# Block 0 of a chunked linear attention with a gated feed-forward: fewer fill-in matrix products, a later fourth q transpose, and two outputs ahead of the first gate product

## The chip, the core and the metric

One core of a Trainium2 chip runs the whole program. The core has a matrix engine (TensorE, "PE" in the profile, with its weight loads as "PEld"), a vector engine (VectorE, "DVE"), a scalar engine (ScalarE, "ACT"), GpSimd ("POOL"), and SyncE ("SP"), which here only issues transfers. Each engine [...] waits on semaphores for the others. The metric is the device time of one execution in microseconds (us); the kernel before takes 224.36 us (median of 6 runs, 223.84 to 224.38).

## The reference

A linear attention with a decay per head runs over blocks of the sequence, and its output is the input of a feed-forward layer with a sigmoid gate:

```python
# q, k, v: (B=4, H=8, S=768, D=64); lam: (8,)
for each block of the sequence:
    intra = (qb @ kb.T * Dmask) @ vb              # Dmask[i, j] = lam ** (i - j) for i >= j
    inter = (qb * lam ** (i + 1)) @ kv_state
    out   = intra + inter
    kv_state = lam ** block * kv_state + (kb * lam ** (block - 1 - i)).T @ vb
x    = out as (B * S = 3072 tokens, H * D = 512)
gate = sigmoid(x @ w_gate)                        # w_gate, w_val: (512, 1536)
y    = (gate * (x @ w_val)) @ w_out               # w_out: (1536, 512), y: (3072, 512)
```

Any block length gives the same result, and the kernel uses 128 positions. In the first block the state is zero, so only the intra part is computed there.

## The kernel before, in words

**Blocks.** The sequence is cut into 6 blocks of 128 positions (`NSTEP`), each for all 4 batches, which gives 512 tokens for the feed-forward per block. A block's attention output is kept transposed as `XT[n]`, 128 partitions x 2 batch pairs x 4 parts of the model dimension x 256 tokens. The feed-forward of a block goes over 12 column tiles of `w_gate` and `w_val` (`piece_gv`, lines 562 to 576): four products for the gate (`gp`), four for the value (`vp`), a tanh on ScalarE, and the product of both on VectorE. Then `piece_po` (line 588) multiplies by `w_out`.

**Block 0.** It is written out by hand in lines 614 to 649, ahead of everything else on TensorE, and it is where the change lies. For each batch b there are these steps:

- `t_0("k", b)` and `t_0("q", b)` (line 282) transpose k and q by eight products with an identity matrix into PSUM. `e_0` (line 337) copies the result to SBUF as `KS` and `QS`, on ScalarE, or on VectorE for q of batches 0 and 1.
- `s_0(b)` (line 291) forms the scores in 16 small products, `sp`; VectorE multiplies them with the decay mask in two instructions (line 304) and writes `MT`.
- `a_0(b, engines)` (line 306) multiplies `MT` with v in 16 small products, `op`, and the engines named copy the result to `XT[0]` (line 320). Batches 0 and 1 are the first half of `XT[0]`, batches 2 and 3 the second.

Ahead of these, `cast_hw` (line 363) turns k of batches 0 and 1, which was loaded in FP32, into bf16 on VectorE. The other loads of q, k, v and the weights are issued from GpSimd's queue, in the order of lines 171 to 198.

**Fill-in products.** `zeros(m, dt)` (line 609) issues m products of zeros, 128 x 512 each, into a PSUM tile that nothing reads. They depend only on the memset of the zeros (line 174).

**First products of the feed-forward.** For the first column tile of block 0 the order is split by halves of `XT[0]`: gate on the first half, value on the first half, gate on the second, value on the second. The gate on the first half is issued by hand at line 647; the other three come from `piece_gv`, with

```python
order = [(gp, WG, first), (vp, WV, first), (gp, WG, second), (vp, WV, second)][1 - n:]
```

which leaves the first entry out for block 0.

**Order.** The order of the instructions on each engine is the order in which they are written. The work behind block 0's attention is a list of units with work attached to each (lines 685 to 804), and nothing in it is touched.

Of the kernel before, what the change touches and what calls it, by code (L numbers as in the profile page):

```python
# [8 lines left out]
FP32 = mybir.dt.float32  # L9
# [7 lines left out]
def kernel(  # L17
# [11 lines left out]
    nc = tc.nc  # L29
# [54 lines left out]
    def rows_of(u):  # L84
        return slice(u * 64, (u + 1) * 64)
# [136 lines left out]
    def powers(w):  # L222
        nc.scalar.activation(mask0[:, w], mask0[:, w], AF.Exp)
# [58 lines left out]
    def t_0(c, b, pool=ps_at, tag="ps"):  # L282
        ps = pool.tile([128, 1, HP, C], BF16, name="t" + c, tag=tag)
        for a in range(2):
            for e in range(2):
                for w in range(2):
                    nc.tensor.transpose(ps[rows_of(w), 0, 2 * a + e, :],
                                        T_[c, 0][:, b, 2 * (2 * a + w) + e, :], ident)
        (tqs if c == "q" else tks)[0, b] = ps

    def s_0(b):
        sp = [ps_at.tile([128, HP, C], FP32, name=f"sp{w}", tag="ps") for w in range(2)]
        for a in range(2):
            for e in range(2):
                for w in range(2):
                    for g in range(2):
                        nc.tensor.matmul(sp[w][rows_of(g), 2 * a + e, :],
                                         lhsT=KS[0, b][rows_of(w), 2 * a + e, rows_of(g)],
                                         rhs=QS[0, b][rows_of(w), 2 * a:2 * a + 2, rows_of(g)],
                                         start=(a == 0 and e == 0), stop=(a == 1 and e == 1),  # L300
                                         skip_group_check=True)
        MT[0, b] = mtp.tile([128, 2, HP, C], BF16, tag="MT", name="MT")
        for w in range(2):
            nc.vector.tensor_tensor(out=MT[0, b][:, w], in0=sp[w], in1=mask0[:, w], op=ALU.mult)

    def a_0(b, engs):
        n = len(engs)
        ops = [ps_at.tile([128, HP // n, C], FP32, name="op", tag="ps") for _ in range(n)]
        for r in range(HP):
            for e in range(2):  # L310
                for g in range(2):
                    o, i = divmod(r, HP // n)
                    nc.tensor.matmul(ops[o][rows_of(g), i, :], lhsT=T_["v", 0][rows_of(g), b, 2 * r + e, :],
                                     rhs=MT[0, b][rows_of(g), r % 2, 2 * (r // 2) + e, :],
                                     start=(i == 0 and e == 0), stop=(i == HP // n - 1 and e == 1),
                                     skip_group_check=True)
        if b == 0:
            new_xt(0)
        for o, eng in enumerate(engs):
            (eng.tensor_copy if eng is nc.vector else eng.copy)(  # L320
                XT[0][:, b // 2, o * (HP // n):(o + 1) * (HP // n), b % 2 * C:(b % 2 + 1) * C], ops[o])
# [15 lines left out]
    def e_0(c, b, eng):  # L337
        es = QS if c == "q" else KS
        if b % 2 == 0:
            t = trsb.tile([128, 2, HP, C], BF16, tag=c.upper() + "S", name=c.upper() + "S")  # L340
            for i in range(2):
                es[0, b + i] = t[:, i]
        (nc.scalar.copy if eng is nc.scalar else nc.vector.tensor_copy)(
            es[0, b], (tqs if c == "q" else tks)[0, b][:, 0])
# [18 lines left out]
    def cast_hw(b):  # L363
        nc.vector.tensor_copy(T_["k", 0][:, b], H32[:, b])
# [52 lines left out]
    def new_xt(n):  # L417
        XT[n] = xtp.tile([128, 2, NMT, TCH // 2], BF16, tag="XT", name="XT")
# [133 lines left out]
    def product(n, ft, ps, W, part):  # L552
        fs = slice(ft * 128, (ft + 1) * 128)
        for mt in range(NMT):
            nc.tensor.matmul(ps[:, part], lhsT=W[:, mt, fs], rhs=XT[n][:, part, mt],  # L555
                             start=(part is not second and mt == 0),
                             stop=(part is not first and mt == NMT - 1), skip_group_check=True)

    def new_gv(n, ft):
        GV[n, ft] = [ps_ff.tile([128, 2, TCH // 2], FP32, name=c, tag="ff") for c in ("gp", "vp")]  # L560
# [48 lines left out]
    def zeros(m, dt=BF16):  # L609
        z = nought if dt is FP32 else ST[1, 0].rearrange("p a h j d -> p (a h j d)")  # L610
        for _ in range(m):
            nc.tensor.matmul(zps, lhsT=z[:, 0:128], rhs=z[:, 0:DM], start=True, stop=True)  # L612
# [2 lines left out]
    powers(0)  # L615
    exponents(1)
    powers(1)
    zeros(2, FP32)
    zeros(3)
    cast_hw(0)  # L620
    cast_hw(1)
    t_0("k", 0)
# [10 lines left out]
    s_0(1)  # L633
    t_0("k", 3, ps_ff, "ff")
    e_0("k", 3, nc.scalar)
    zeros(1)
    for b in range(2, 4):
        t_0("q", b)
        e_0("q", b, nc.scalar)
    zeros(1)  # L640
    s_0(2)
    a_0(0, (nc.scalar,))
    a_0(1, (nc.scalar,))
    s_0(3)
    zeros(1)
    new_gv(0, 0)
    product(0, 0, GV[0, 0][0], WG, first)
    a_0(2, (nc.scalar,))
    a_0(3, (nc.scalar, nc.vector))

# [182 lines left out]
```

## Time and profile before

| What | us |
|---|---|
| device time, median of 6 runs | 224.36 |
| device time of the profiled execution | 224.34 |
| its span, first to last instruction | 222.6 |
| PE busy | 216.8 |
| ACT busy | 107.9 |
| DVE busy | 103.7 |
| POOL busy | 64.7 |

The profiled execution is one of the same kernel with the hardware profiler on; its span lies inside its device time, with 1.74 us around it. Starts in the lines of the timeline are in us from the start of the span. In a merged line the second number is the time from the first start to the last end, and "x8" means eight instructions. The ends of products are modelled, with about 0.2 us of pipeline behind the last start, so that lines overlap. The number in brackets is the idle time of the engine just before, with what ended it.

### The profile page before, as it was taken

To read this page: it belongs to the slowest core of one execution; us is meant where nothing else is said; L and a number is where in the kernel's file an instruction comes from. 1 tells how busy PE (TensorE), PEld (TensorE's weight loads), DVE (VectorE), ACT (ScalarE), POOL (GpSimd) and SP (SyncE) were. 2 spreads that over 40 slices of the span, in tenths; PEclk is the share of its full clock that TensorE was granted. 3 is DMA by queue.
4 is the path that set the end of the run, shared out by engine and by line. 5 is a ranking of instruction groups with operands and counts; after the bars stand their busy time and mean duration, and the time that the engine had idled before them with its cause. 6 is when DMAs were issued, how large, how long until landed. Compare 5 with 4: busy or idle time off the path is not lost.

```text
span 222.6 us, 5459 instructions
## 1 busy us (share of the span) xinstructions
PE 216.8 (97%) x2310; PEld 107.6 (48%) x2310; DVE 103.7 (47%) x192; ACT 107.9 (48%) x236; POOL 64.7 (29%) x85
## 2 busy tenths in 40 slices
PE   7989999999999999999999999999999999999994
PEld 2564444557444544444544444544444544444443
DVE  4854575539777501785700785700676400333300
ACT  5748764594384523385433376342366342333221
POOL 7999755740392008402910030000000000000000
PEclk9999999999999999999999999999999999999999
DMA  6999999999899999997999994012100012100022
GB/s 116 177 179 185 196 199 182 167 156 158 140 86 158 255 209 155 181 195 95 98 159 200 210 67 32 3 50 94 47 3 0 0 53 94 47 0 1 3 94 96
DMA packets 99401, 25.27 MB, mean 114 GB/s; under 512 B 90032, under 2 KB 96432, under 8 KB 99376
## 3 DMA queue, kind: packets, MB, share of 16 engines
q0 software_dynamic: 77872, 13.90, 78.0%
q1 hardware_dynamic: 20688, 10.69, 19.9%
q10 hardware_dynamic: 816, 0.33, 0.6%
q8 instruction: 18, 0.29, 0.5%
q14 instruction: 7, 0.06, 0.1%
HBM read 28.32 MB, written 6.29 MB: 155 GB/s over the span
## 4 chain that ended last, share of the span: by engine, by line
PE 92%; POOL 4%; DMA 3%; issue 1%; ACT 0%; POOLq 0%
PE po L595 28%; PE gp L555 28%; PE vp L555 28%; DMA WV<-in_moe_w_val_dram 3%; POOL vb L114 1%; PE sp L455 1%; PE cp L515 1%; PE op L479 1%; POOL qb L114 1%; PE op L493 1%; POOL kb L114 1%; PE sp L381 0%; PE op L412 0%; PE tk L279 0%; PE tq L279 0%
## 5 line engine op out<-in xcount | busy, mean ns | idle before, releaser
L550 DVE SCALAR_TENSOR_TENSOR ht<-sg,vp 128x512 bf16<-128x512 f32 x72 | 49.4, 686 | 93.1 <-PE vp L555 87.4
L555 PE MATMUL vp<-XT,WV 128*128 128x512 bf16 (+1 forms) x296 | 74.3, 373 | 0.7 <-DMA WV<-in_moe_w_val_dram 0.7
L555 PE MATMUL gp<-XT,WG 128*128 128x512 bf16 (+1 forms) x296 | 74.3, 373 | 0.2 <-ACT XT L320 0.2
L573 ACT ACTIVATE sg<-gp 128x512 f32<-128x512 f32 x72 | 43.0, 597 | 59.4 <-PE gp L555 59.4
L595 PE MATMUL po<-WO,ht 128*128 128x512 bf16 (+2 forms) x300 | 63.9, 371 | 0.0
L555 PEld LDWEIGHTS <-WV 128*128 128x128 bf16 x296 | 28.9, 98 | 34.1 <-DMA WV<-in_moe_w_val_dram 0.9
L595 PEld LDWEIGHTS <-ht 128*128 128x128 bf16 x300 | 28.3, 98 | 31.9
L555 PEld LDWEIGHTS <-WG 128*128 128x128 bf16 x296 | 28.2, 98 | 31.7 <-issue 0.4
L599 ACT ACTIVATE ob<-po 128x512 f32<-128x512 f32 (+1 forms) x24 | 14.0, 583 | 38.6 <-PE po L595 38.6
L143 ACT ACTIVATE kd<-kb,kds 128x128 bf16<-128x128 bf16 x80 | 25.2, 389 | 0.0
L674 POOL COPY gates<-qt 128x1 bf16<-128x1 bf16 x4 | 1.5, 386 | 50.0 <-DMA qt<-qb 50.0
L505 ACT CAST XT<-op 128x512 bf16<-128x512 f32 x16 | 8.2, 600 | 5.0 <-PE op L493 5.0
L465 DVE TENSOR_TENSOR MT<-sp,mask 128x512 bf16<-128x512 f32 x16 | 10.3, 682 | 0.0
L96 POOL DMA_DIRECT2D vb<-in_v_dram x6 | 9.0, 1503 | 3.0 <-issue 1.4
L102 POOL DMA_DIRECT2D qb<-in_q_dram x10 | 8.8, 893 | 2.9 <-DMA WO<-in_moe_w_out_dram 2.9
L102 POOL DMA_DIRECT2D kb<-in_k_dram x10 | 9.0, 919 | 1.0 <-DMA WG<-in_moe_w_gate_dram 0.6
L612 PE MATMUL zps<-st 128*128 128x512 bf16 (+1 forms) x10 | 6.2, 748 | 1.5 <-DVE st L174 1.5
L121 POOL DMA_DIRECT2D WV<-in_moe_w_val_dram x9 | 7.4, 836 | 0.0
L118 POOL DMA_DIRECT2D WG<-in_moe_w_gate_dram x8 | 6.8, 848 | 0.0
L540 DVE SCALAR_TENSOR_TENSOR st<-st,pow_l,cp 128x128 bf16<-128x128 bf16 x24 | 6.7, 342 | 0.0
L96 POOL DMA_DIRECT2D kb<-in_k_dram x5 | 5.9, 1184 | 1.2 <-DMA WG<-in_moe_w_gate_dram 1.2
L96 POOL DMA_DIRECT2D qb<-in_q_dram x5 | 5.8, 1153 | 0.5 <-DMA WO<-in_moe_w_out_dram 0.5
(93 smaller groups left out, 125.5 us busy)
## 6 DMA issues: line engine op xcount, KB each, us to landing
out_dram<-ob SPq DMA_DIRECT2D x19, 256.0 KB, 2.0
vb<-in_v_dram POOLq DMA_DIRECT2D x4, 512.0 KB, 7.0
qb<-in_q_dram POOLq DMA_DIRECT2D x14, 128.0 KB, 7.5
kb<-in_k_dram POOLq DMA_DIRECT2D x12, 128.0 KB, 9.1
WO<-in_moe_w_out_dram POOLq DMA_DIRECT2D x4, 384.0 KB, 12.1
kb<-in_k_dram POOLq DMA_DIRECT2D x5, 256.0 KB, 8.9
qb<-in_q_dram POOLq DMA_DIRECT2D x5, 256.0 KB, 8.4
WG<-in_moe_w_gate_dram POOLq DMA_DIRECT2D x4, 256.0 KB, 7.0
```

The source lines that it names most:

```text
L96: nc.gpsimd.dma_start(out=T_[c, n][:, b0:nat], in_=src[b0:nat, :, sl, :].rearrange("b h s d -> s (b h) d"))
L102: nc.gpsimd.dma_start(out=T_[c, n][:, m:b1, u::2, :], in_=src[m:b1, 1 - u::2, sl, :].rearrange("b h s d -> s (b h) d"))
L118: nc.gpsimd.dma_start(out=WG[:, :, f0 * 128:f1 * 128], in_=wg_r[:, :, f0 * 128:f1 * 128])
L121: nc.gpsimd.dma_start(out=WV[:, :, f0 * 128:f1 * 128], in_=wv_r[:, :, f0 * 128:f1 * 128])
L143: nc.scalar.mul(KD[n][:, at, i, :], T_["k", n][:, at, i, :], kds[:, min(n // FIRST_XBAR, 1), h:h + 1])
L465: nc.vector.tensor_tensor(out=MT[n, bp][:, u], in0=SP[n, bp][u], in1=mask[:, u ^ bp].unsqueeze(1).to_broadcast([128, 2, HP, L]), op=ALU.mult)
L505: nc.scalar.copy(XT[n][:, bp].rearrange("p m (j c i) -> p m j c i", j=2, c=2)[:, :, :, c, :], OP[n, c, bp])
L550: return nc.vector.scalar_tensor_tensor(out=o, in0=g, scalar=1.0, in1=x, op0=ALU.add, op1=ALU.mult)
L555: nc.tensor.matmul(ps[:, part], lhsT=W[:, mt, fs], rhs=XT[n][:, part, mt], start=(part is not second and mt == 0), stop=(part is not first ...
L573: nc.scalar.activation(sg, gp.rearrange("p a b -> p (a b)"), AF.Tanh, scale=0.5)
L595: nc.tensor.matmul(po[:, :c1 - c0], lhsT=HT[n, ft][:, tt * 128:(tt + 1) * 128], rhs=WO[:, ft, c0:c1], start=(ft == 0), stop=(ft == NFT - 1))
L599: (eng.mul if eng is nc.scalar else eng.tensor_scalar_mul)(o, po[:, :c1 - c0], 0.5)
```

## The change

Four things change, all between lines 614 and 649:

- At the start, two FP32 and three bf16 fill-in products become one FP32 product.
- Two of the later fill-in products, one on each side of the q transposes of batches 2 and 3, are gone. The last one, behind `s_0(3)`, stays.
- The transposes of q of batch 3, with their copy, move from ahead of `s_0(2)` to behind it.
- `a_0(2)` and `a_0(3)`, with their copies, move ahead of the gate product on the first half.

```diff
@@ -615,8 +615,7 @@
     powers(0)
     exponents(1)
     powers(1)
-    zeros(2, FP32)
-    zeros(3)
+    zeros(1, FP32)
     cast_hw(0)
     cast_hw(1)
     t_0("k", 0)
@@ -633,20 +632,19 @@
     s_0(1)
     t_0("k", 3, ps_ff, "ff")
     e_0("k", 3, nc.scalar)
-    zeros(1)
-    for b in range(2, 4):
-        t_0("q", b)
-        e_0("q", b, nc.scalar)
-    zeros(1)
+    t_0("q", 2)
+    e_0("q", 2, nc.scalar)
     s_0(2)
+    t_0("q", 3)
+    e_0("q", 3, nc.scalar)
     a_0(0, (nc.scalar,))
     a_0(1, (nc.scalar,))
     s_0(3)
     zeros(1)
+    a_0(2, (nc.scalar,))
+    a_0(3, (nc.scalar, nc.vector))
     new_gv(0, 0)
     product(0, 0, GV[0, 0][0], WG, first)
-    a_0(2, (nc.scalar,))
-    a_0(3, (nc.scalar, nc.vector))
```

No load, no work of GpSimd and no order of instructions on VectorE or ScalarE is different; the order changes on TensorE alone.

## The prediction

> **What bounds the kernel now.** I read the page first: TensorE is busy for 97% of the span. Then the waits of TensorE from 15 us to the end, to see whether anything behind the changed stage could absorb a shift.
>
> ```profile
> span 222.6 us, 5459 instructions
> PE 216.8 (97%) x2310; PEld 107.6 (48%) x2310; DVE 103.7 (47%) x192; ACT 107.9 (48%) x236; POOL 64.7 (29%) x85
> ```
>
> ```profile
> PE vp L555 <- DMA WV<-in_moe_w_val_dram: 0.7, 1, 0.7
> ```
>
> The second fence is the whole answer: behind 15 us TensorE waits once, 0.7 us, for the first tile of `w_val`. From there to its last product it doesn't wait again. So the start of the first value product is a gate: what delays it delays the end by as much, and nothing that only makes work ahead of it earlier gains anything. The timeline of TensorE up to there:
>
> ```profile
> 1.53 5.06 PE L612 MATMUL zps<-st 128*128 128x512 f32 x7 [1.53 <-DVE st L174]
> 6.68 0.64 PE L287 MATMUL tk<-ident,kb 128*64 128x128 bf16 x8
> 7.20 0.43 PE L287 MATMUL tq<-ident,qb 128*64 128x128 bf16 x8
> 7.45 0.41 PE L287 MATMUL tk<-ident,kb 128*64 128x128 bf16 x8
> 7.67 0.41 PE L287 MATMUL tq<-ident,qb 128*64 128x128 bf16 x8
> ...
> 12.76 0.39 PE L612 MATMUL zps<-st 128*128 128x512 bf16 x1
> 13.31 0.60 PE L555 MATMUL gp<-XT,WG 128*128 128x256 bf16 x4 [0.16 <-ACT XT L320]
> 13.84 1.08 PE L313 MATMUL op<-MT,vb 64*64 64x128 bf16 x32
> 15.65 0.61 PE L555 MATMUL vp<-XT,WV 128*128 128x256 bf16 x4 [0.73 <-DMA WV<-in_moe_w_val_dram]
> ```
>
> The chain of work that ended last says when the `w_val` tile came: its transfer runs from 9.66 for 5.94 us, to 15.60.
>
> ```profile
> 9.66 5.94 DMA WV<-in_moe_w_val_dram
> ```
>
> And the mask multiplications on VectorE, which feed the outputs:
>
> ```profile
> 8.66 2.48 DVE L304 TENSOR_TENSOR MT<-sp,mask 128x512 bf16<-128x512 f32 x4
> 11.68 2.48 DVE L304 TENSOR_TENSOR MT<-sp,mask 128x512 bf16<-128x512 f32 x4 [0.53 <-PE sp L297]
> ```
>
> **The pace of TensorE.** The timeline shows a second thing. The first eight transposes keep the engine from 6.68 to 7.20, 0.52 us; the same eight later take 0.25 and 0.22. The fill-in products agree: in narrow windows of the timeline the FP32 ones start at 1.53, 2.54, 3.40 and 4.25 (two per product, 0.85 apart), the bf16 ones at 5.53 and 5.96, 0.43 apart for 512 columns, while the four whole gate products later take 0.86, or 0.215 each. So TensorE runs at half pace until about 7.2 us and at full pace from there. The listing of the fill-in line shows the extremes:
>
> ```profile
> L612 PE MATMUL zps<-st x10: 389/634/1222, 1.5 to 12.8; 128*128 128x512 bf16 x6, 128*128 128x512 f32 x4
> ```
>
> A bf16 product takes 389 ns late and 634 ns early. The clock column reads 1.00 in these first windows, so the change of pace has to be read from the starts.
>
> [...]
>
> **The change part by part.**
>
> *Fill-in at the start.* Removed: one FP32 (2 x 0.85) and three bf16 products (3 x 0.43), 3.0 us at half pace. As work they cost nothing: the first transpose waits for the cast of k, which ends at 6.66 (6.20 plus one of two casts of 0.46). The remaining product ends at about 3.3, and TensorE idles from there to 6.66. The removal frees nothing[...]. So I take half pace from 6.68 on[...]. That is the price of this edit.
>
> *Fill-in in the middle.* Two bf16 products, 0.22 us each at full pace. They stood in the queue ahead of the q transposes and of the third scores. Removing them, with the fourth q moved back (another 0.22), lets the third scores start up to 0.2 us earlier: ScalarE's copy of q had 0.17 us of idle time. Everything gained is ahead of the gate at 15.60: worth 0.
>
> *Outputs ahead of the gate product.* Before, the first gate product (0.44 us) ran at 13.31, in the time in which v of batches 2 and 3 was still under way (issued up to 9.06, 4.6 us to landing, 13.7). Now it comes behind the last output. At full pace: outputs of batch 2 from 13.7, batch 3 done at about 14.65, gate product to 15.1, half a microsecond ahead of `w_val`. Cost 0, but the cover shrinks: what delays the last output by more than 0.5 us is now paid in full, where before there was 0.73.
>
> *Half pace through the attention.* Eight transposes or 16 scores take 0.43 instead of 0.22, 16 outputs 0.86 instead of 0.44, and a result is ready 0.2 us behind that. Durations on the other engines are those of before (copies 0.56 to 0.64, mask pair 1.25, two pairs 2.48). Replayed in the new order, with the waits on the copies:
>
> - k0, q0, k1, q1 at 6.68, 7.11, 7.54, 7.97, to 8.40; the scores of batch 0 8.40 to 8.83, before 8.14.
> - k2 to 9.26, scores of batch 1 to 9.69, k3 to 10.12, q2 to 10.55. VectorE's first four multiplications 9.1 to 11.6.
> - ScalarE copies k2 at 9.5, k3 at 10.4 and q2 at 10.95, done 11.5. Third scores 11.55 to 11.98, multiplied 12.25 to 13.5 (before from 11.68).
> - q3 to 12.41, outputs of batches 0 and 1 to 14.13, fourth scores to 14.56, their result 14.8, multiplied 14.8 to 16.08 (before to 14.16).
> - Fill-in to 14.99, outputs of batch 2 to 15.85; outputs of batch 3 wait for 16.08 and end at 16.96.
> - Gate product on the first half 0.44 at full pace: the value product starts at 17.40. That is 17.40 - 15.65 = 1.75 us late.
>
> No transfer is late there, since all were due for 15.65 and the chain has none behind it. So the end moves by 1.75.
>
> *When the clock turns.* Turned by 12.0, the fourth scores end by 13.35, the last mask at 14.8, the gate product at about 15.7: 0.1 late. Turned at 14.1: last mask 15.9, gate product done 16.85, 1.2 late. At 17.0: 1.75. From there each further us costs 0.5, because the gate stage then runs at half pace.
>
> [...] Scores and outputs become dense only at about 11.55[...]. I take 17: 1.75 us.
>
> **Sum.** 0 for the removed work, 0 for the two moves, 1.75 for the clock: span 222.6 + 1.75 = 224.35, and with the 1.74 around the span 226.1. The profiled execution (224.34) stands at the median (224.36), so no correction.
>
> **Rivals.**
>
> *The pace turns in time, or the delay is hidden.* The transposes and scores from 6.68 to 10.55 keep TensorE occupied without a gap. [...] then the gate at 15.60 hides it all: 224.2 to 224.5. This is the rival that isn't slower; it decides at 12.0 us, as worked out above. [...]
>
> *Only the gate products turn it.* The small products use 64 x 64 tiles [...]: 227.8 to 229.5, middle 228.6. [...] Against: transposes and small products did hold the pace from 7.2 to 13.
>
> *A gain.* The middle fill-ins and the fourth q held the third scores. It would need the value product ahead of 15.65, so an earlier `w_val`; its queue is GpSimd's, whose order is the same, and its transfers run without a gap. Bound: 223.9.
>
> **How the numbers follow.** Turned at 13 to 19 us: 0.57, 225.0 to 227.1, with 226.1 the likeliest. In time or hidden: 0.14. Late: 0.23. A gain of over 0.2%: 0.06. The least that a measurement of this kernel tells from no change is about 0.2%, 0.45 us. The first and third case are slower, 0.80; the second is within, 0.14. The range leaves the gain, part of the hidden case and the upper half of the late case out: 224.3 to 228.6.
>
> **What would show it.** Right: transposes of k0, q0, k1, q1 start 0.43 apart; the third scores near 11.55; the last mask ends near 16; the value product starts near 17.4 with no wait for `w_val`; gate products take 0.86 from there. Hidden: the starts tighten to 0.22 before 12 us, and the wait for `w_val` at 15.60 is still there. Late: four gate products take 1.7 us for a stretch. Wrong altogether: full pace at 7.2 as before[...].

## The result

The changed kernel takes 225.77 us (median of 18 runs, 224.71 to 226.75) against 224.40 us before (median of 40 runs, 223.84 to 224.58): a ratio of 1.0064, with a 95% interval of 1.0050 to 1.0077. It is slower by about 1.4 us. But no execution took the median's time: nine lie between 224.71 and 225.16 (the earlier group, median 224.99) and nine between 226.39 and 226.75 (the later group, median 226.62). Against 224.40 that is 0.6 and 2.2 us. The profiled execution (224.99, span 223.2) is one of the earlier group.

The page after, its span and busy times:

```profile
span 223.2 us, 5445 instructions
PE 214.6 (96%) x2303; PEld 107.6 (48%) x2303; DVE 103.5 (46%) x192; ACT 108.0 (48%) x236; POOL 63.5 (28%) x85
```

TensorE is busy for 2.2 us less, and the span is 0.6 us longer. All waits of TensorE after (total, count, longest):

```profile
PE tk L287 <- DVE kb L364: 3.0, 1, 3.0
PE zps L612 <- DVE st L174: 1.5, 1, 1.5
PE sp L297 <- ACT QS L343: 0.8, 1, 0.8
PE op L313 <- DVE MT L304: 0.3, 1, 0.3
```

The wait for `w_val` is gone: the value product no longer waits for data, the attention has become the bound. The timeline of TensorE after:

```profile
1.53 2.08 PE L612 MATMUL zps<-st 128*128 128x512 f32 x2 [1.53 <-DVE st L174]
6.64 0.64 PE L287 MATMUL tk<-ident,kb 128*64 128x128 bf16 x8 [3.03 <-DVE kb L364]
7.11 0.64 PE L287 MATMUL tq<-ident,qb 128*64 128x128 bf16 x8
7.51 0.67 PE L287 MATMUL tk<-ident,kb 128*64 128x128 bf16 x8
7.93 0.67 PE L287 MATMUL tq<-ident,qb 128*64 128x128 bf16 x8
...
10.67 0.56 PE L287 MATMUL tq<-ident,qb 128*64 128x128 bf16 x8
12.04 0.42 PE L297 MATMUL sp<-QS,KS 64*64 64x128 bf16 x16 [0.82 <-ACT QS L343]
...
15.43 0.52 PE L313 MATMUL op<-MT,vb 64*64 64x128 bf16 x12 [0.29 <-DVE MT L304]
15.88 0.61 PE L555 MATMUL gp<-XT,WG 128*128 128x256 bf16 x4
16.33 0.60 PE L555 MATMUL vp<-XT,WV 128*128 128x256 bf16 x4
```

The starts of the first four transposes are 0.47, 0.40 and 0.42 apart, where before the third and fourth followed after 0.25 and 0.22. Half pace lasts until the q transposes at 10.67, which end a little early (0.56 against 0.64). The value product starts at 16.33 instead of 15.65, 0.68 late, and the span is 0.6 longer. The mask multiplications on VectorE after, which end at 15.37 instead of 14.16:

```profile
9.28 2.48 DVE L304 TENSOR_TENSOR MT<-sp,mask 128x512 bf16<-128x512 f32 x4 [0.22 <-PE sp L297]
12.49 1.29 DVE L304 TENSOR_TENSOR MT<-sp,mask 128x512 bf16<-128x512 f32 x2 [0.73 <-PE sp L297]
14.08 1.29 DVE L304 TENSOR_TENSOR MT<-sp,mask 128x512 bf16<-128x512 f32 x2 [0.30 <-PE sp L297]
```

The chain that ended last now runs through the attention, where before it ran through GpSimd's queue and the transfer of `w_val`. Its piece ahead of the third scores (start, us, what):

```profile
10.92 0.58 ACT KS L343
11.51 0.50 ACT QS L343
12.04 0.42 PE sp L297 x16
```

ScalarE copies k of batch 3 and then q of batch 2; TensorE has nothing to do from 11.2 to 12.04. This hole matters below.

### The profile page after: what moved, and what is told of

The parts are those of the page before. It is cut to its first block, busy times and chain, and to the rows that moved or that the text cites. A ratio compares the mean times of both kernels' runs of the same rounds, so it can differ in the third digit from the quotient of the medians.

```text
span 223.2 us, 5445 instructions
## 1 busy us (share of the span) xinstructions
PE 214.6 (96%) x2303; PEld 107.6 (48%) x2303; DVE 103.5 (46%) x192; ACT 108.0 (48%) x236; POOL 63.5 (28%) x85
## 4 chain that ended last, share of the span: by engine, by line
PE 95%; DMA 2%; DVE 1%; ACT 1%; ACTq 0%; issue 0%; DVEq 0%
PE gp L555 28%; PE po L595 28%; PE vp L555 28%; DMA h<-in_k_dram 2%; PE sp L455 1%; PE cp L515 1%; PE op L479 1%; PE op L493 1%; PE tk L287 1%; PE sp L297 1%; PE op L313 1%; DVE MT L304 1%; PE tq L287 1%; PE sp L381 0%; PE op L412 0%; PE tk L279 0%
## 5 line engine op out<-in xcount | busy, mean ns | idle before, releaser
L672 POOL COPY gates<-qt 128x1 bf16<-128x1 bf16 x4 | 0.7, 186 | 48.1 <-DMA qt<-qb 48.1
L465 DVE TENSOR_TENSOR MT<-sp,mask 128x512 bf16<-128x512 f32 x16 | 10.2, 681 | 0.0
L389 DVE TENSOR_TENSOR MT<-sp,mask 128x512 bf16<-128x512 f32 x8 | 5.0, 682 | 1.9 <-PE sp L381 1.9
```

The lines of the kernel that those rows point to most:

```text
L465: nc.vector.tensor_tensor(out=MT[n, bp][:, u], in0=SP[n, bp][u], in1=mask[:, u ^ bp].unsqueeze(1).to_broadcast([128, 2, HP, L]), op=ALU.mult)
```

## The experiments

The theory: behind the fill-in products of the start TensorE had full pace ahead of the attention (from 7.27 us of the span before, by the trace's clock record); without them the attention runs at half pace (to 11.00 us after), and the whole loss follows from that. The rivals: the new order costs, or the middle fill-ins do.

### The start put back

```diff
 (the changed kernel)
-    zeros(1, FP32)
+    zeros(2, FP32)
+    zeros(3)
```

> The changed kernel with all five fill-in products at the start put back; the order and the middle stay as changed. Theory of the clock: the removed start is the whole loss, so full pace from about 7.2 us, the value product waits for w_val again and starts at 15.6 to 15.7, and the time is 224.2 to 224.5, with all executions within 0.7 us. Rival, the order costs (gate product behind the last output): the value product starts later than 16 us and the time stays at 225 or above.

224.46 us (224.29 to 225.58, 14 runs), ratio 1.0002, interval 0.9994 to 1.0011. The whole loss is gone, with the new order in place: the clock is the cause, the order alone costs nothing measurable. One of the 14 executions lay outside, at 225.58; its mean clock on record is 0.990, against 0.998 to 1.000 in the others, which would be about 4 us back at half pace (an estimate from the mean, with half pace as a granted clock of 0.5, which the record after has behind its stretch of full pace; there is no trace of it). But the timeline of TensorE shows that the order used up the cover:

```profile
10.26 0.41 PE L287 MATMUL tq<-ident,qb 128*64 128x128 bf16 x8 [0.34 <-DMA qb<-in_q_dram]
11.35 0.42 PE L297 MATMUL sp<-QS,KS 64*64 64x128 bf16 x16 [0.67 <-ACT QS L343]
...
14.73 0.52 PE L313 MATMUL op<-MT,vb 64*64 64x128 bf16 x12 [0.16 <-DVE MT L304]
15.18 0.61 PE L555 MATMUL gp<-XT,WG 128*128 128x256 bf16 x4
15.87 0.61 PE L555 MATMUL vp<-XT,WV 128*128 128x256 bf16 x4
```

The third scores start at 11.35, not earlier than the 11.23 of before, because the third q comes by transfer only at 10.26. The fourth q then stands ahead of the outputs, and the last outputs start at 14.73. The gate product of 0.44 ends at 15.62, only 0.25 us ahead of the value product at 15.87.

### The start cut in the kernel before

```diff
 (the kernel before)
-    zeros(2, FP32)
-    zeros(3)
+    zeros(1, FP32)
```

> The kernel before with the start cut to one FP32 product, everything else as before. Theory of the clock: half pace from 6.7 us, executions in two groups as with the change, the earlier at most 0.5 us above the kernel before (the gate product is hidden again ahead of the outputs), the later 1.5 to 2.5 above, median 224.7 to 226.2. Rival, the order costs: as the kernel before, 224.2 to 224.5.

225.00 us (224.30 to 225.41, 20 runs), ratio 1.0022, interval 1.0015 to 1.0029. Slower, as the clock wants it, but by 0.5 us, and the later group is missing: not one of 20 executions beyond 225.41. The median lies in the range expected, but the two groups that were expected are not there. The profile fell on one of the three fastest executions (224.33). Its scores and transposes are at full pace from about 9.9 us, and its value product starts at 15.53, no later than before:

```profile
9.29 0.64 PE L287 MATMUL tk<-ident,kb 128*64 128x128 bf16 x8
9.86 0.42 PE L297 MATMUL sp<-QS,KS 64*64 64x128 bf16 x16
...
15.53 0.61 PE L555 MATMUL vp<-XT,WV 128*128 128x256 bf16 x4
```

No profile shows the slower ones. Three things differ from the changed kernel: two fill-ins in the middle, the fourth q, and the gate product.

### No fill-in at the start

```diff
 (the changed kernel)
-    zeros(1, FP32)
```

> The changed kernel without any fill-in product at the start. Theory of the clock[...]: the one FP32 product was worth nothing, so the same two groups, 224.7 to 225.2 and 226.4 to 226.8, median anywhere between. Rival, [...] more executions in the later group, median at or above 226.4, or a third group above 227.

225.12 us (224.71 to 227.04, 17 runs): ten executions between 224.71 and 225.19, seven between 226.59 and 227.04. The same two groups; the one FP32 product that the change keeps at the start makes no difference to be told (ten of 17 in the earlier group without it, nine of 18 with it).

### The middle fill-ins alone taken out

```diff
 (the kernel before)
-    zeros(1)
     for b in range(2, 4):
         t_0("q", b)
         e_0("q", b, nc.scalar)
-    zeros(1)
```

> The kernel before without its two fill-in products around the q transposes; start and order as before. Theory of the clock: full pace from about 7.2 us, the third scores up to 0.2 us earlier, the value product still at 15.6 to 15.7 behind the wait for w_val: 224.2 to 224.5, no difference. Rival, the middle fill-ins hold the clock up: a time above 225 in part of the executions.

224.47 us (223.87 to 224.63, 13 runs), ratio 0.9996, interval 0.9988 to 1.0004. With the start in place the middle ones are worth nothing. Nor do the third scores start earlier (11.29); in the timeline of TensorE a wait for q has taken the place of the fill-in:

```profile
10.20 0.64 PE L287 MATMUL tq<-ident,qb 128*64 128x128 bf16 x16 [0.40 <-DMA qb<-in_q_dram]
11.29 0.42 PE L297 MATMUL sp<-QS,KS 64*64 64x128 bf16 x16 [0.45 <-ACT QS L343]
```

### The gate product back ahead of the outputs

```diff
 (the changed kernel)
+    new_gv(0, 0)
+    product(0, 0, GV[0, 0][0], WG, first)
     a_0(2, (nc.scalar,))
     a_0(3, (nc.scalar, nc.vector))
-    new_gv(0, 0)
-    product(0, 0, GV[0, 0][0], WG, first)
```

> The changed kernel with the first gate product back ahead of the outputs of batches 2 and 3; the start stays cut. Theory: the clock costs and the place of the gate product adds up to its own 0.44 us, so both groups of executions come 0.3 to 0.44 us earlier than with the change: about 224.5 and 226.2. Rival, the clock alone: no difference from the change.

225.08 us (224.77 to 226.48, 7 runs): four executions at 224.77 to 225.08 and three at 226.34 to 226.48. Both groups stay, their medians some 0.15 and 0.26 us below those of the change (224.85 and 226.36 against 224.99 and 226.62). That is half of what was expected, from few runs, and within the spread of the groups themselves: the place of the gate product is a small part of the loss at most.

### Two FP32 products at the start

```diff
 (the changed kernel)
-    zeros(1, FP32)
+    zeros(2, FP32)
```

> The changed kernel with two FP32 products at the start, 3.4 us of work from 1.53 to about 4.95. [...] about a third of the executions at 224.3, the rest in the two groups of the change. [...] If the FP32 work counts less than the transposes, no execution gains.

224.98 us (224.37 to 226.67, 10 runs): three executions at 224.37 to 224.47, four at 224.86 to 225.06, three at 226.15 to 226.67. About a third gain, as expected, and no other work than FP32 products of zeros stood ahead of full pace in the profile (224.46, full pace from 5.66 us). Ten runs are few for shares. Two of the last three (226.15 and 226.20) seem to be of another kind than the later group of the change: their mean clocks on record are 0.985 and 0.983, where all executions of the change have 0.998 or more. That would be about 7 us back at half pace after a first stretch at full pace (an estimate from the mean, with a granted clock of 0.5; there is no trace of them).

### The middle fill-ins put back

```diff
 (the changed kernel)
+    zeros(1)
     t_0("q", 2)
     e_0("q", 2, nc.scalar)
+    zeros(1)
     s_0(2)
```

> The changed kernel with one fill-in product ahead of the third q transpose and one ahead of the third scores put back; the start stays cut, the order stays changed. Theory: the later group of executions comes from the 0.8 us in which TensorE waits for the copy of the third q[...]. The fill-in shortens that gap to about 0.4 us, so the later group shrinks or goes away, all or nearly all executions at 224.7 to 225.5. Rival, only the start matters: the two groups of the change, about half at 226.4 to 226.8.

225.19 us (224.90 to 227.37, 8 runs): five executions at 224.90 to 225.34, two at 225.8, one at 227.37. The group at 226.4 to 226.8 is gone but for that one, and something in between has appeared. Its profile (225.78) shows in the timeline of TensorE what the fill-in does there:

```profile
10.98 0.61 PE L612 MATMUL zps<-st 128*128 128x512 bf16 x1
11.52 0.64 PE L287 MATMUL tq<-ident,qb 128*64 128x128 bf16 x8
12.08 0.61 PE L612 MATMUL zps<-st 128*128 128x512 bf16 x1
12.83 0.42 PE L297 MATMUL sp<-QS,KS 64*64 64x128 bf16 x16
```

The fill-ins run at half pace themselves and delay the third scores to 12.83, but they close the hole, and the clock turns at 12.6. They cost their own length and, in all but one of these 8 executions, the long delay is gone.

### A profile of the later group

The changed kernel was profiled twice more, without an edit.

> The changed kernel once more, to have a profile of the later group of its executions (half of them). If it falls there: half pace until about 14.5 us, fourth scores and last mask late by more than 1 us against the profile at hand, value product at about 17.9. If it falls in the earlier group: as the profile at hand.

225.07 us: the earlier group, with full pace from 11.16 us and nothing else new.

> The changed kernel once more, for a profile of the later group of its executions. If it falls there: half pace until between 13.5 and 15.5 us, last mask later than 16 us, value product between 17.5 and 18.2, and no pace below full behind 18 us. If it falls in the earlier group: half pace until between 9 and 12 us, value product at 16.0 to 16.6.

227.21 us, span 225.4: the later group. Its attention starts 0.54 us later by itself, since the cast of k did; without that it would lie at 226.67, inside the group. The timeline of TensorE:

```profile
12.66 0.64 PE L297 MATMUL sp<-QS,KS 64*64 64x128 bf16 x16 [0.74 <-ACT QS L343]
13.80 1.70 PE L313 MATMUL op<-MT,vb 64*64 64x128 bf16 x28
...
16.61 0.75 PE L313 MATMUL op<-MT,vb 64*64 64x128 bf16 x20 [0.47 <-issue]
...
17.98 0.61 PE L555 MATMUL gp<-XT,WG 128*128 128x256 bf16 x4
18.43 0.60 PE L555 MATMUL vp<-XT,WV 128*128 128x256 bf16 x4
```

The 28 outputs take 1.70 us, where after they took 0.97: half pace through the fourth scores. Full pace begins at 16.56, later than expected, and the value product starts at 18.43, or 17.89 without the late start. The gate products are at full pace.

### The work ahead of full pace

The trace file of an execution holds a clock record with the moment of full pace; the clock column of the views reads 1.00 ahead of it too. Two traces have no such record (the start cut in the kernel before, and the gate product back). From the span's start the moment is 7.27 us before, 11.00 after, 11.38 without any fill-in, 12.57 with the middle put back, 5.66 with two FP32 products, 16.56 in the later group. In each of the twelve records full pace lasts a whole multiple of 3.413 us (61 to 64 of them; 215.040 us, or 63, before, and 211.626 us, or 62, after), so stretches of that length can be laid back from the moment of full pace. That TensorE's busy time in such a stretch decides is a reading of these traces. Where the stretches lie differs from execution to execution: with the same five products from 1.53 us on, six profiles (before, the start put back, the middle taken out, and the three versions further down) have full pace from between 4.96 and 7.34.

TensorE's busy time in each stretch (columns: stretch, length, busy time and number of instructions, then clock, DMA share and GB/s), in the later group:

```profile
6.32:9.73 3.41, 2.54 (x50) 1.00 1.80 177
9.73:13.15 3.42, 2.68 (x60) 1.00 1.81 178
13.15:16.56 3.41, 2.99 (x63) 1.00 1.81 180
```

The third of these stretches is fuller than it reads. Of the fill-in product behind the fourth scores the trace has the weight load, at 16.07, but no record of the product itself; the only products of that line are the FP32 ones of the start:

```profile
L612 PE MATMUL zps<-st x2: 1061/1140/1220, 1.5 to 2.5; 128*128 128x512 f32 x2
L612 PEld LDWEIGHTS <-st x1: 105/105/105, 16.1 to 16.1; 128*128 128x128 bf16 x1
```

The "idle" 0.47 us ahead of 16.61 stands in its place. Such a product takes 0.61 us at half pace (the middle put back), so this stretch was full, or nearly.

After, in the earlier group:

```profile
4.18:7.59 3.41, 0.95 (x18) 1.00 1.67 197
7.59:11.00 3.41, 3.41 (x76) 1.00 1.80 177
```

With two FP32 products at the start:

```profile
2.25:5.66 3.41, 3.06 (x4) 1.00 1.07 195
```

Behind the stretches with 2.54 and 2.68 us of work (74% and 78%) half pace went on, and behind the one with 3.06 (90%) came full pace. Before, half pace went on behind a stretch with 2.33 us, and full pace came behind the next, with 3.32:

```profile
0.44:3.86 3.42, 2.33 (x3) 1.00 0.31 64
3.86:7.27 3.41, 3.32 (x15) 1.00 1.62 214
```

So none of these stretches with up to 78% of busy time has full pace behind it, and those with 90% and more have it; in between lies only the third of the later group, whose 88% is too low a reading. The stretch from 7.59 to 11.00 holds transposes and scores alone, and full pace came behind it. The scores are two blocks of 0.57 us in it, a third of the stretch; without the transposes it would be emptier than those that half pace followed, so by this reading the transposes count.

An estimate from these figures accounts for the groups. A stretch that takes in the hole from 11.22 to 12.04 whole is at most 76% full. If 10% to 22% of a stretch may be idle (0.34 to 0.75 us, from the 90% and the 78%), full pace comes either behind a stretch that ends at the latest that far into the hole, by 11.6 to 12.0, or behind one that starts at the earliest that far ahead of the hole's end, and then not before 14.7 to 15.1. Which of the two depends on where the stretches lie. With work from 6.64 to 11.22, stretches that start between 6.30 and 8.15 are full enough at 10% idle, an estimate of 54% of all placements, and 78% of them at 22% idle; 23 of 42 executions (the change, no fill-in, and the gate product back) were in the earlier group, which is 55%. The account fits, but only three executions of the changed kernel have a trace.

### Versions against both kernels

Before, TensorE waited for `w_val` with the second gate product still to do. Three kernels put the first tile's gate product on both halves ahead of the value products, each with the full start:

```diff
         if ft == 0 and n <= 1:
             order = [...]
+        if ft == 0 and n == 0:
+            order = [(gp, WG, second), (vp, WV, first), (vp, WV, second)]
```

On the kernel before, with no other edit:

> The kernel before with one edit: the gate product of the first tile on both halves ahead of the value products. The second gate product can start when the last copy ends, at 15.4, and runs in the time in which the first value product waited for w_val until 15.65: 0.25 us less than before, 224.1 to 224.3. Rival, no difference: 224.4.

224.30 us, ratio 1.0001, interval 0.9992 to 1.0009: no difference to be told. On the changed kernel with the start put back:

> The changed kernel with all five fill-in products at the start, and the gate product of block 0's first tile on both halves ahead of the value products. With the clock at full pace the last copy of the output comes at about 15.2, the second gate product fits ahead of the arrival of w_val at 15.6, and both value products follow: 0.3 to 0.45 us less than the kernel before, 223.9 to 224.1. Rival, the transfer of w_val comes later in the same measure or the copies end later than 15.4: 224.2 to 224.5.

224.26 us, ratio 0.9996, interval 0.9988 to 1.0004: not told apart either. On the kernel before with the last two outputs ahead of the gate product, as the change has them:

> The kernel before with its fill-in and its order of the q transposes, but the last two outputs ahead of the gate product as in the change, and the gate product of the first tile on both halves ahead of the value products. Theory: the last mask ends at 14.2 as before, the last copy at 15.2, both gate products end at 15.6, when w_val arrives: 0.45 us less than before, 223.9 to 224.1. Rival, the outputs end at 14.9 as before and the gate products behind them: the value product starts at 16.0 and the gain is 0.1 or less.

224.07 us (223.96 to 224.24, 13 runs), ratio 0.9990, interval 0.9982 to 0.9998. This is ahead of both kernels, of the one before by 0.2 to 0.3 us (224.41 us beside it), with an interval that just leaves out 1. The first of the three versions, which ran beside it and differs only in the place of the outputs, took 224.30 us (224.12 to 224.76). Its timeline of TensorE:

```profile
13.71 1.08 PE L313 MATMUL op<-MT,vb 64*64 64x128 bf16 x31 [0.38 <-DMA vb<-in_v_dram]
14.72 1.17 PE L555 MATMUL gp<-XT,WG 128*128 128x256 bf16 x8
15.72 1.04 PE L555 MATMUL vp<-XT,WV 128*128 128x256 bf16 x8
```

The outputs end at 14.72, both gate products fit ahead of `w_val`, and the two value products follow without a break. So one part of the change, the place of the outputs, is worth something once there is other work to put behind it.

## Why the prediction was right or wrong

**Right: the mechanism.** The price of the change is that of the clock, and the removed start carries it. With the start back, the loss is gone (1.0002). With the start cut in the kernel before, a loss appears (1.0022). The value product was rightly taken as the gate: it is 0.68 us late after, and the span 0.6 us longer. The measured 225.77 lies 0.3 below the 226.1 forecast and inside the range, but that it is so near is luck: it is the middle between 225.16 and 226.39, the edges of two groups of equal size, and no execution comes within 0.6 us of it. The likeliest case, half pace through the whole attention, is what the later group shows (full pace from 16.56).

**Wrong: one case where there are two.** The forecast gave the moment of full pace one likeliest value, 17 us. It is 11.00 in one profile and 16.56 in the other. I took "turned in time" as a rival of 0.14, while the earlier group, whose two profiles have full pace from 11.00 and 11.16, is half of the executions (nine of 18). The 17 and the 0.14 rested on an assumption of mine that no trace or run had shown, that transposes do little to bring full pace. The measurement decides against it: after, the 3.41 us ahead of full pace (7.59 to 11.00) hold transposes and scores alone, and two thirds of that are these products with an identity matrix.

**Mis-sized: the decision point.** "Turned by 12.0" was to be hidden but for 0.1 us. Turned at 11.00 it costs 0.68; only the 9.9 of the start cut in the kernel before was hidden, in that kernel's order. The term that was too small is the length of a block at half pace. The eight transposes and 16 scores were put at 0.43 each; where scores and transposes alternate, the starts are 0.57 apart (8.53, 9.10, 9.67, 10.24 after), so the third scores start at 12.04 instead of 11.55. The profile before had shown the like at full pace, where blocks of changing kind start 0.34 to 0.35 apart and not 0.22:

```profile
9.03 0.42 PE L297 MATMUL sp<-QS,KS 64*64 64x128 bf16 x16
9.38 0.41 PE L287 MATMUL tk<-ident,kb 128*64 128x128 bf16 x8
9.72 0.39 PE L612 MATMUL zps<-st 128*128 128x512 bf16 x1
```

So each change from one kind to the other adds 0.12 to 0.15 us at either pace, which the replay left out. And the later group's value product, at 17.89 without its late start, is 0.5 behind the 17.40 of the replay, by the same term.

**Wrong: what the middle is worth.** "Worth 0" holds only with the start in place (0.9996). With the start cut, the middle fill-ins close the hole: in 28 executions with them (the start cut in the kernel before, and the middle put back) one lay beyond 226 us, in 42 without them 19 did. The edit was priced against the pace of the kernel before and not against the pace that the other edit leaves behind. The start cut in the kernel before differs in order too, so the share that is theirs is best read from the middle put back, with only 8 runs; that the order has a part in it is not ruled out.

**Wrong: the third scores up to 0.2 us earlier.** The 0.17 us of ScalarE's idle time was taken for room. The third q arrives at 10.1 to 10.3, and without the fill-in TensorE waits for it for 0.34 to 0.40 us. This changed no sum.

**Wrong: the cover of half a microsecond.** At full pace the outputs were to end at 14.65 and the gate product at 15.1. They end at 15.18 and 15.62, since the fourth q stands in front of the outputs of batch 0. The move costs nothing measurable at full pace (1.0002). At half pace the gate product's own part in the loss is 0.15 to 0.26 us by the medians, which is within the spread of the groups.

**The rivals.** "Only the gate products turn it" is out: in neither group's profile is a gate product at half pace (the first four take 0.61 us in both, and before 0.60), and the forecast 227.8 to 229.5 was reached by no execution of any kernel. The gain didn't appear.

**Open.** Why alternating blocks take longer was not tried; each changes the tile, from 128*64 to 64*64 or back. Whether a stretch with between 78% and 90% of busy time would have full pace behind it was not measured, and it stays open whether busy time is what decides: that of the trace holds a modelled end of about 0.2 us ahead of each gap. What put the three executions at 225.58, 226.15 and 226.20 back at half pace, if that is what their mean clocks say, is not known.

## What to carry to other kernels

Ask of idle-looking filler work what state it leaves behind, and of a hole in TensorE's work whether it comes while the engine is still at half pace; here a hole of 0.8 us went with a loss of 0.6 us in the executions with full pace ahead of it (from 11.00 in the profile), and of 2.2 us in those with full pace late (from 16.56). Price two edits that touch the same state together: the middle fill-ins were worth nothing with the first ones in place, and without these they go with the later group all but missing. And look at the list of executions before the median: where it falls in two groups, the median is no execution's time.

## What the hardware showed

- In these traces full pace came behind 3.413 us in which TensorE was busy for 3.06 us (90%, two FP32 products), 3.32 (before) or 3.41 (after), and half pace went on behind 2.33 us (before), 2.54 and 2.68 us (74% and 78%, the later group). The moment differs between executions with the same work ahead of it (4.96 to 7.34 us in six profiles).
- 3.41 us of transposes and scores, two thirds of it transposes, had full pace behind them (after, 7.59 to 11.00).
- Two FP32 products of zeros, with 3.06 us of work in the 3.413 us, had full pace behind them at 5.66 us.
- One FP32 product, 1.7 us of work with nothing behind it, changed nothing (9 of 18 executions in the earlier group with it, 10 of 17 without).
- Blocks of transposes and scores that alternate take 0.12 to 0.15 us more each than blocks of one kind in a row, at half pace (0.57 against 0.40 to 0.43) and at full pace (0.34 to 0.35 against 0.22).
